# Placing the negated row maxima of an attention kernel: a TensorE transpose replaced by VectorE's 32x32 block transpose

## The chip, the cores and the metric

The kernel runs on one NeuronCore of a Trainium2 chip. The metric is the device time of one execution in microseconds (us), given as the median of several runs; lower is better. One further execution was recorded by the hardware profiler, and all traces below are of such an execution. TensorE appears in it as PE (matmuls) and PEld (weight loads), VectorE as DVE, ScalarE as ACT, GpSimd as POOL, and SyncE, which issues nearly all DMAs, as SP.

## The reference

All data are float32. One sequence of 2048 rows with 640 columns goes through two branches, which are mixed by a gate per row:

```python
g = sigmoid((x * gate_w).sum(-1))            # one number per row
q, k, v = split(x @ wqkv)                    # 32 heads of 20 columns
p = softmax(q @ k.T * 20 ** -0.5)            # per head, 2048 x 2048
a = (p @ v) @ wo
b = Cr @ (x @ Dr.T) - Ci @ (x @ Di.T)        # Fourier mixing, real part
out = g * a + (1 - g) * b
```

The weights are scaled so that scores are large: the exponential needs the maximum of each row subtracted. The change concerns how these maxima get into the matrix product whose result is exponentiated.

## The kernel before

**Units.** Attention runs in 32 units. A unit is a pair of heads and one half (1024) of the query rows. The two heads, h = 0 and h = 1, lie in the partitions from 0 and from 64 of the same tiles, so that two matmuls with few rows can run side by side. Scores are needed twice. The first pass (`s_mm`, L197, "m" in the order strings) computes a 128-query by 512-key block into a PSUM bank, and VectorE reduces it to 128 maxima (L199). The second pass (`score`, L949, "e") computes the block the other way round, 128 keys by 512 queries, and ScalarE exponentiates it (L951). The second pass uses 62 rows in place of 60: the rows 60 and 61 of a head's query stack hold the negated maximum of each query in two parts, a float32r value and the remainder, and the key stack holds ones there. So the matmul itself subtracts the maxima. Then the weights meet V (`av_step`, L556) in bursts of 16 or 24 matmuls.

**The chain of one unit.** `s_end` notes that a unit's first pass is done. `max_nm` (L213) reduces its maxima once more on VectorE to the tile `nm`: 128 partitions (the query within a block of 128) by 16 columns (head times 8 blocks), negated. `max_chain` has to lay these 128 x 16 numbers into rows of 1024 queries. Before, a matmul with the identity (L231) turns `nm` into 16 x 128 in a PSUM bank taken from the common rotation `bank()`, two VectorE operations (the helper `split`, L115 and L116) make the parts `m1` and `m2` of it, and `rows()` issues four DMAs on SP that place eight partitions of `m1` or `m2` as one row of 4 KB. From the first pass of a unit to its second there are 41 steps (`LEAD`), a step being one "e" for each of the two heads; a unit has 32 steps.

**What sets the order.** All engines work in program order; the order is written out by hand. In the long middle part, a cycle of six steps follows the second string of `ORDERS`: "e" and "m" are blocks of the two passes, "F" fills in matmuls of the Fourier branch (L635), and "B" is the burst, which first calls `run_extras` and `run_casts` (among them ScalarE's cast L113, whose remainder GpSimd then computes at L116), then the AV matmuls L556, and between or after them `max_chain`. The tuples behind the string tell which of the two heads comes first in a step: for "e" `(0, 0, 0, 1, 0, 1)`. Blocks of both passes take their PSUM banks in turn from five places of one rotation, so a block must wait until the block five places earlier has been read. The DMAs of `rows()` stand in SP's queue two steps after the chain; SP waits there, and everything behind it waits too.

**The parts of the span.** Up to about 217 us there are projections without chains; to about 600 us Fourier work of the hidden axis (L378) fills in, in cycles of four steps; to about 1650 us Fourier work of the sequence (L635), in cycles of six steps; then the output projection (L742). Units are numbered 0 to 31; unit 0's chain runs at 217 us, those of 1 to 7 stand in the second part, 8 to 28 in the third, 29 to 31 in the last.

Of the kernel before, what the change touches and what calls it, by code (L numbers as in the profile page):

```python
# [11 lines left out]
F32 = mybir.dt.float32  # L12
R = mybir.dt.float32r
# [6 lines left out]
P = 128  # L20
# [9 lines left out]
KROWS = 3 * DH  # L30
# [42 lines left out]
def f32(ap):  # L73
    return ap.bitcast(F32)
# [3 lines left out]
def mix_kernel(ctx: ExitStack, tc: tile.TileContext, xa, wqk, wb, cdft, wo, out):  # L78
    nc = tc.nc
    pe, act, dve, pool, sp = nc.tensor, nc.scalar, nc.vector, nc.gpsimd, nc.sync  # L80
    ctx.enter_context(tc.manual_schedule())

    def pools(**kw):
        return ctx.enter_context(tc.tile_pool(**kw))

    const = pools(name="const", bufs=1)
    small = pools(name="small", bufs=1)
# [13 lines left out]
    ident = const.tile([P, P], F32, name="ident")  # L101
# [9 lines left out]
    def split(dst1, dst2, src, e1, e2):  # L111
        if e1 is act:
            act.activation(dst1, src, AF.Copy)  # L113
        else:
            e1.tensor_copy(dst1, src)  # L115
        e2.tensor_tensor(dst2, src, f32(dst1), op=ALU.subtract)  # L116
# [8 lines left out]
    def place_tile(name):  # L125
        return ps_w.tile([P, 512], F32, name=name)

    def bank():
        places.rotate(-1)
        return place_tile(places[-1])  # L130
# [45 lines left out]
    def q_unit(n):  # L176
        p, u = VISITS[n]
        return third["q"] if p == 14 else qst[place(p)][:, u * (S // 2) : (u + 1) * (S // 2)]

    mx, nms, ends = {}, {}, []  # L180
    now, later = [-1], {}

    def at_step(i, fn):
        later.setdefault(i, []).append(fn)
# [16 lines left out]
    def s_end(i):  # L201
        n, s = divmod(i, 32)
        if n < NU and s == 31:
            if now[0] < 0:
                max_nm(n)
            else:
                ends.append(n)
        if s == 1 and 0 < n <= NU and now[0] < 0:
            max_chain(n - 1)
# [17 lines left out]

    def max_chain(n):
        q = q_unit(n)
        pt = bank()[:16, :P]  # L230
        pe.matmul(pt, nms.pop(n), ident, start=True, stop=True)  # L231
        m1 = small.tile([16, P], R, name="m1")
        m2 = small.tile([16, P], R, name="m2")
        split(m1, m2, pt, dve, dve)

        def rows():
            for h in range(2):
                b = 64 * h + KROWS
                sp.dma_start(f32(q[b : b + 1, :]), f32(m1[8 * h : 8 * h + 8, :]))
                sp.dma_start(f32(q[b + 1 : b + 2, :]), f32(m2[8 * h : 8 * h + 8, :]))  # L240

        if now[0] < 0:
            rows()
        else:
            at_step(now[0] + 2, rows)
# [578 lines left out]
    start = 4 * HID  # L824
# [130 lines left out]
    def burst(c):  # L955
        ready = any(n in nms for n in ends)
        for n in ends:
            if n not in nms:
                max_nm(n)
        k, _, i = phase(c)  # L960
        steps = 6 if k == 1 else 4
        run_extras(steps - 2)
        if k == 1:
            run_casts()
        for kt in range(i // 2, (i + steps) // 2):
            if ready and kt == (i + steps) // 2 - 1:
                max_chain(ends.pop(0))
            av_step(now[0], kt // NS, kt % NS, kt % NS == 0 and kt > i // 2)
        while ends:
            max_chain(ends.pop(0))  # L970
        if c in (HID - NS - 1, HID - 1):
            next_pool()
# [134 lines left out]
```

## Time and profile before

| | |
|---|---|
| Median of 3 runs | 1854.2 us (1853.94 to 1856.85) |
| Span of the profiled execution, first to last instruction | 1852.1 us |
| Mean granted TensorE clock | 0.999 |
| Busy: PE, PEld | 1844.1, 1365.3 us |
| Busy: DVE, ACT, POOL | 1379.7, 1357.0, 1003.6 us |
| Matmuls L231 | 64 records, 12.2 us |
| VectorE split of the turned maxima, L115 and L116 on `m` | 32 + 32, 8.8 + 8.9 us |
| Row DMAs L239 and L240 | 128 issues |

An engine's busy time is the time in which at least one of its instructions runs, waits inside an instruction included. A float32 matmul by the identity is recorded as two matmuls, hence 64 for 32 units. A row of a timeline gives the start in us from the span's start, the duration of the merged instructions, the engine, the line, and how many were merged; brackets give the idle time ahead and what ended it. A row of a group gives the count, then the minimum, median and maximum duration in ns. SP's instructions are issues of DMAs; their durations are the time the issuing takes, not the transfer.

### The profile page before, as it was taken

The numbers are of one execution on the slowest core, as the hardware profiler recorded it, in microseconds if no ns is written. First come the engines' busy times: TensorE is split into PE (matmuls) and PEld (weight loads), VectorE is DVE, ScalarE is ACT, GpSimd is POOL, SyncE is SP. The second block draws the span as 40 slices with busy tenths as digits, with TensorE's granted clock in tenths as the row PEclk, the third lists the DMA queues.
The fourth block names the chain that finished last, engine by engine and source line by source line (L and its number), as shares of the span: only waits on it lengthen the run. The fifth ranks groups of instructions, "written<-read, shape, count | busy, mean of one in ns | idle before, by whom it ended". The sixth has DMA issues, their size and how long they took to land.

```text
span 1852.1 us, 44874 instructions
## 1 busy us (share of the span) xinstructions
PE 1844.1 (100%) x17638; PEld 1365.3 (74%) x17638; DVE 1379.7 (74%) x2309; ACT 1357.0 (73%) x2645; POOL 1003.6 (54%) x832
## 2 busy tenths in 40 slices
PE   9999999999999999999999999999999999999998
PEld 8988777676776777777777777777777777776666
DVE  3044458888787888888888888888888888888853
ACT  4222258878787888888788888888888877778885
POOL 4334432121136676344677788655668767645644
PEclk9999999999999999999999999999999999999999
DMA  7744341222135574636566586646475856531233
GB/s 236 173 136 157 136 126 56 79 64 67 58 92 149 200 215 148 157 118 194 177 201 227 159 261 197 192 140 183 130 235 189 246 163 206 178 91 55 82 99 109
DMA packets 178771, 281.61 MB, mean 152 GB/s; under 512 B 44811, under 2 KB 113547, under 8 KB 178559
## 3 DMA queue, kind: packets, MB, share of 16 engines
q1 hardware_dynamic: 177599, 276.77, 49.1%
q0 software_dynamic: 960, 1.97, 0.6%
q8 instruction: 138, 2.26, 0.5%
q14 instruction: 74, 0.61, 0.1%
HBM read 214.61 MB, written 63.52 MB: 150 GB/s over the span
## 4 chain that ended last, share of the span: by engine, by line
PE 99%; DMA 0%; DVE 0%; ACT 0%; POOL 0%; SPq 0%; issue 0%; POOLq 0%; ACTq 0%
PE ps L556 25%; PE yp L635 19%; PE ps L949 17%; PE ps L197 14%; PE yp L378 7%; PE ps L119 4%; PE ps L120 4%; PE ps L121 4%; PE yp L742 3%; DMA p<-in_xa 0%; PE ps L231 0%; DVE mx L199 0%; PE ps L1041 0%; POOL x L1010 0%; PE yp L1062 0%
## 5 line engine op out<-in xcount | busy, mean ns | idle before, releaser
L199 DVE TENSOR_REDUCE mx<-ps 128x1 f32<-128x512 f32 x2048 | 1280.6, 684 | 305.8 <-PE ps L197 235.8
L951 ACT ACTIVATE p<-ps 128x512 f32<-128x512 f32 x2048 | 1055.1, 612 | 282.4 <-PE ps L197 159.3
L949 PE MATMUL ps<-qst,kst 62*128 62x512 f32 x1920 | 727.7, 406 | 0.2
L197 PE MATMUL ps<-kst,qst 60*128 60x512 f32 x1920 | 664.3, 409 | 0.0
L635 PE MATMUL yp<-x,part 64*128 64x320 f32 x5376 | 628.1, 306 | 0.0
L635 PEld LDWEIGHTS yp<-x,part 64*128 64x128 f32 x5376 | 601.7, 186 | 5.2
L556 PE MATMUL ps<-p,v 128*21 128x512 f32 (+1 forms) x4096 | 482.0, 595 | 0.0
L116 POOL TENSOR_TENSOR part<-raw,part 128x1024 fp32r<-128x1024 f32 (+1 forms) x128 | 287.4, 2246 | 338.3 <-ACT part L113 322.4
L949 PEld LDWEIGHTS ps<-qst,kst 62*128 62x128 f32 x1920 | 341.3, 185 | 155.5 <-DVE mx L199 86.4
L197 PEld LDWEIGHTS ps<-kst,qst 60*128 60x128 f32 x1920 | 323.3, 184 | 11.8 <-issue 4.2
L556 PEld LDWEIGHTS ps<-p,v 128*21 128x21 f32 (+1 forms) x4096 | 104.8, 101 | 236.1 <-issue 228.6
L378 PE MATMUL yp<-wb,x 64*128 64x320 f32 x1920 | 223.9, 307 | 0.0
L378 PEld LDWEIGHTS yp<-wb,x 64*128 64x128 f32 x1920 | 209.8, 186 | 6.5 <-ACT raw L388 0.2
L389 POOL TENSOR_TENSOR raw<-raw 128x320 f32<-128x320 f32 x64 | 55.6, 869 | 267.0 <-ACT raw L388 210.0
L515 POOL TENSOR_TENSOR raw<-raw,raw 128x1024 f32<-128x1024 f32 x77 | 187.4, 2434 | 1.5 <-DMA raw<-in_cdft 1.5
L113 ACT ACTIVATE part<-raw 128x1024 fp32r<-128x1024 f32 (+2 forms) x121 | 123.4, 1020 | 2.0 <-DMA raw<-in_wqk 1.9
L742 PE MATMUL yp<-x,part 64*128 64x320 f32 x768 | 102.2, 308 | 0.0
L116 POOL TENSOR_TENSOR x<-araw,x 128x320 fp32r<-128x320 f32 x112 | 97.4, 877 | 1.3
L338 ACT ACTIVATE p<-ps 128x512 f32<-128x512 f32 x40 | 23.7, 597 | 100.1 <-PE ps L121 97.1
L742 PEld LDWEIGHTS yp<-x,part 64*128 64x128 f32 x768 | 92.0, 186 | 1.3
L119 PE MATMUL ps<-x,part 128*128 128x512 f32 x200 | 79.9, 400 | 0.5 <-ACT x L113 0.3
L120 PE MATMUL ps<-x,part 128*128 128x512 f32 x200 | 78.6, 393 | 0.4 <-DVE x L116 0.4
(101 smaller groups left out, 1364.2 us busy)
## 6 DMA issues: line engine op xcount, KB each, us to landing
raw<-in_cdft SPq DMA_DIRECT2D x192, 512.0 KB
araw<-a_scr SPq DMA_DIRECT2D x192, 160.0 KB
qk_scr<-p SPq DMA_DIRECT2D x40, 512.0 KB
kst<-qk_scr SPq DMA_DIRECT2D x84, 160.0 KB
qst<-qk_scr SPq DMA_DIRECT2D x84, 160.0 KB
yt<-y_scr SPq DMA_DIRECT2D x80, 160.0 KB
a_scr<-raw SPq DMA_DIRECT2D x64, 160.0 KB
y_scr<-yt SPq DMA_DIRECT2D x64, 160.0 KB
```

Of the source, the lines that this page charges most:

```text
L116: e2.tensor_tensor(dst2, src, f32(dst1), op=ALU.subtract)
L119: pe.matmul(ps, st1, mv1, start=first, stop=False)
L120: pe.matmul(ps, st1, mv2, start=False, stop=False)
L197: pe.matmul(ps, q[b : b + KROWS, qt * P : (qt + 1) * P], k[b : b + KROWS, kc * 512 : (kc + 1) * 512], start=True, stop=True)
L199: return lambda: dve.tensor_reduce(mx[n][:, h, qt, kc : kc + 1], ps, axis=AX.X, op=ALU.max)
L378: pe.matmul(yp[h][:, :HE], x[r, xz, d, cs], w[r, wz, d, :HE], start=d == 0 and z == 0, stop=d == ND - 1 and z == 2)
L515: pool.tensor_tensor(raws[0], raws[0], raws[1], op=ALU.add if PRODUCTS[n][0][1][0] > 0 else ALU.subtract)
L556: pe.matmul(t[32 * j : 32 * j + m, :], v[:, r : r + m], pp[qc][:, h, :], start=kt == 0, stop=kt == NS - 1)
L635: pe.matmul(yp[h][:, :HE], c[r, cz, cs], a[r, az], start=s == 0 and z == 0, stop=s == NS - 1 and z == 2)
L742: pe.matmul(yp[h][:, :HE], o[oz][r], wos[d, hf][r, wz], start=d == 0 and z == 0, stop=end)
L949: pe.matmul(pt, k[b : b + KROWS + 2, kt * P : (kt + 1) * P], q[b : b + KROWS + 2, qc * 512 : (qc + 1) * 512], start=True, stop=True)
L951: act.activation(pts[n, kt, qc][:, h], pt, AF.Exp, scale=float(DH) ** -0.5)
```

## The change

The maxima are no longer turned by TensorE. `max_chain` splits `nm` where it lies, in SBUF with its 128 partitions, into a tile `mt` of 128 x 32 (head, part, block of queries), and VectorE's block transpose turns each of the four 32 x 32 squares into `mtt`. A partition of `mtt` then holds 32 queries of one head, part and block. Eight DMAs place them: for each head h and each group b of 32 partitions, sixteen pieces of 128 bytes go to the two rows of the head.

```diff
     def max_chain(n):
         q = q_unit(n)
-        pt = bank()[:16, :P]
-        pe.matmul(pt, nms.pop(n), ident, start=True, stop=True)
-        m1 = small.tile([16, P], R, name="m1")
-        m2 = small.tile([16, P], R, name="m2")
-        split(m1, m2, pt, dve, dve)
+        t, tt = [small.tile([P, 32], F32, name=name) for name in ("mt", "mtt")]
+        parts = t.rearrange("p (h z c) -> p h z c", h=2, z=2).bitcast(R)
+        split(parts[:, :, 0], parts[:, :, 1], nms.pop(n).rearrange("p (h c) -> p h c", h=2), dve, dve)
+        dve.transpose(tt, t)
 
         def rows():
             for h in range(2):
-                b = 64 * h + KROWS
-                sp.dma_start(f32(q[b : b + 1, :]), f32(m1[8 * h : 8 * h + 8, :]))
-                sp.dma_start(f32(q[b + 1 : b + 2, :]), f32(m2[8 * h : 8 * h + 8, :]))
+                dst = f32(q[64 * h + KROWS : 64 * h + KROWS + 2, :]).rearrange("z (t b c) -> z t b c", t=8, b=4)
+                for b in range(4):
+                    r = 32 * b + 16 * h
+                    sp.dma_start(dst[:, :, b], tt[r : r + 16])
```

Outside the 32 chains the order of the instructions on every engine is the same; the rotation of banks advances by one place less per unit. The next rows show VectorE's queue at the chain of unit 10, from `nm` to the first reductions behind the chain (L199 reads a block's bank, `ps`). Before:

```order
L213 TENSOR_REDUCE nm<-mx 128x16
L199 TENSOR_REDUCE mx<-ps_10498 128x1
L199 TENSOR_REDUCE mx<-ps_10501 128x1
L199 TENSOR_REDUCE mx<-ps_10507 128x1
L199 TENSOR_REDUCE mx<-ps_10510 128x1
L115 CAST m_10526<-ps_10524 16x128
L116 TENSOR_TENSOR m_10527<-ps_10524,m_10526 16x128
L199 TENSOR_REDUCE mx<-ps_10539 128x1
```

Now:

```order
L213 TENSOR_REDUCE nm<-mx 128x16
L199 TENSOR_REDUCE mx<-ps_10528 128x1
L199 TENSOR_REDUCE mx<-ps_10531 128x1
L199 TENSOR_REDUCE mx<-ps_10537 128x1
L199 TENSOR_REDUCE mx<-ps_10540 128x1
L115 CAST mt<-nm 128x2x8
L116 TENSOR_TENSOR mt<-nm,mt 128x2x8
L233 STREAM_TRANSPOSE mtt<-mt 128x32
L199 TENSOR_REDUCE mx<-ps_10568 128x1
```

The chain keeps its place among the reductions; it is three instructions in place of two, and its inputs are `nm` and `mt` in SBUF in place of a PSUM bank `ps`.

SP's queue at the same unit, where `m_10526` and `m_10527` are the parts `m1` and `m2`. Before:

```order
L580 DMA r_scr<-lc 128x16
L239 DMA qst_89<-m_10526 1x8x128
L240 DMA qst_89<-m_10527 1x8x128
L239 DMA qst_89<-m_10526 1x8x128
L240 DMA qst_89<-m_10527 1x8x128
L510 DMA raw<-in_cdft 128x1024
L584 DMA rb<-r_scr 32x512 x4
```

Now:

```order
L580 DMA r_scr<-lc 128x16
L240 DMA qst_89<-mtt 2x8x32 x8
L510 DMA raw<-in_cdft 128x1024
L584 DMA rb<-r_scr 32x512 x4
L775 DMA y_scr<-m 128x320 x2
L891 DMA kst_86<-qk_scr 20x4x512
```

Eight issues stand where four stood, h = 0 first, and the loads behind them are unchanged.

TensorE's queue at the same place (L556 the burst, `ps_10524` the bank of the turned maxima). Before:

```order
L556 MATMUL ps_9893<-p,v 21x512 x8
L231 MATMUL ps_10524<-ident,nm 16x128
L556 MATMUL ps_9893<-p,v 21x512 x4
L949 MATMUL ps_10536<-qst_88,kst_86 128x512
L197 MATMUL ps_10539<-kst_87,qst_89 128x512
```

Now the row L231 is gone and the twelve rows of L556 stand together; the blocks behind them follow in the same order.

## The prediction

> **What bounds the kernel now.** First the page's busy times and its chain of waits:
>
> ```profile
> PE 1844.1 (100%) x17638; PEld 1365.3 (74%) x17638; DVE 1379.7 (74%) x2309; ACT 1357.0 (73%) x2645; POOL 1003.6 (54%) x832
> PE 99%; DMA 0%; DVE 0%; ACT 0%; POOL 0%; SPq 0%; issue 0%; POOLq 0%; ACTq 0%
> ```
>
> TensorE sets the end. A busy PE is no proof, since its ends are modelled, so I read PE's timeline next, for the starts of the bursts L556 in cycles of six steps, without a chain (672.19 to 681.49, 728.47 to 737.76) and with one.
>
> ```profile
> 672.19 2.77 PE L556 MATMUL ps<-p,v 128*21 128x512 f32 x24
> 681.49 2.77 PE L556 MATMUL ps<-p,v 128*21 128x512 f32 x24
> 684.08 0.38 PE L231 MATMUL ps<-ident,nm 128*16 128x128 f32 x2
> 691.26 0.63 PE L556 MATMUL ps<-p,v 128*21 128x512 f32 x4
> ...
> 728.47 2.77 PE L556 MATMUL ps<-p,v 128*21 128x512 f32 x24
> 737.76 1.91 PE L556 MATMUL ps<-p,v 128*21 128x512 f32 x16
> 739.49 0.27 PE L231 MATMUL ps<-ident,nm 128*16 128x128 f32 x1
> 740.66 0.49 PE L949 MATMUL ps<-qst,kst 62*128 62x512 f32 x1
> 742.24 0.39 PE L949 MATMUL ps<-qst,kst 62*128 62x512 f32 x1
> 745.55 0.39 PE L949 MATMUL ps<-qst,kst 62*128 62x512 f32 x1
> 747.26 1.06 PE L556 MATMUL ps<-p,v 128*21 128x512 f32 x8
> ```
>
> A cycle without a chain takes 9.30 us (681.49 - 672.19), a fixed beat; with a chain inside the burst 9.50 (747.26 - 737.76), with one behind the burst 9.77 (691.26 - 681.49). So PE has no slack that could take up a new wait, and each L231 costs it a time that can be read off.
>
> **What the change removes.** The transposes' rows:
>
> ```profile
> L231 PE MATMUL ps<-ident,nm x64: 272/273/283, 217.3 to 1782.3; 128*16 128x128 f32 x64
>   DVE nm L213: 8.4, 18
>   DVE mx L199: 4.3, 14
> ```
>
> The 14 are chains inside a burst (units 8, 10, 11, 13 and so on), 0.20 us each, 2.8 in all. The 18 are seven behind bursts of six steps (9, 12 and so on to 27; 0.47, so 3.3), one of unit 0 with two waits, and ten behind bursts of four steps (1 to 7, 29 to 31), for which I take 0.20 too: 2.3. The 0.47 holds 0.20 for the matmuls; the rest comes later in that cycle, from the turned maxima's place in the bank rotation, which goes too. **Gain: 8.4 us.**
>
> **What it puts on VectorE.** The split now has 16 elements in each of 128 partitions. Neighbours by size:
>
> ```profile
> L457 DVE TENSOR_SCALAR ngate<-gate x1: 177/177/177, 121.3 to 121.3; 128x16 f32<-128x16 f32 x1
> L213 DVE TENSOR_REDUCE nm<-mx x32: 207/216/221, 217.0 to 1779.8; 128x16 f32<-128x64 f32 x32
> L1057 DVE COPY rb<-lc x1: 427/427/427, 1836.5 to 1836.5; 128x512 f32<-128x512 f32 x1
> 739.91 0.28 DVE L115 CAST m<-ps 16x128 fp32r<-16x128 f32 x1
> 740.23 0.28 DVE L116 TENSOR_TENSOR m<-ps,m 16x128 fp32r<-16x128 f32 x1
> 741.23 1.91 DVE L199 TENSOR_REDUCE mx<-ps 128x1 f32<-128x512 f32 x3 [0.72 <-PE ps L197]
> ```
>
> I take 0.17 for the cast, 0.18 for the subtraction, 0.20 for the block transpose (no row has one: 0.18 to 0.43, near the small ones) and 0.04 behind each, together 0.67 us against 0.59 before. By itself that is nothing: VectorE idles 0.72 us behind the chain of unit 10.
>
> But two operations change the memory they read, and the trace has a row on what that can cost. First the group of a subtraction with both inputs in SBUF, then two of its members and what GpSimd ran beside them:
>
> ```profile
> L116 DVE TENSOR_TENSOR wb<-raw,wb x8: 815/1166/2151, 18.1 to 117.7; 128x966 fp32r<-128x966 f32 x4, 128x644 fp32r<-128x644 f32 x4
> 115.58 2.15 DVE L116 TENSOR_TENSOR wb<-raw,wb 128x966 fp32r<-128x966 f32 x1 [3.28 <-ACT wb L113]
> 115.40 1.30 POOL L116 TENSOR_TENSOR p<-p 128x512 fp32r<-128x512 f32 x1
> 19.83 1.35 DVE L116 TENSOR_TENSOR wb<-raw,wb 128x644 fp32r<-128x644 f32 x1 [0.50 <-ACT wb L113]
> 18.40 2.09 POOL L116 TENSOR_TENSOR p<-p 128x512 fp32r<-128x512 f32 x1
> ```
>
> An operation that takes about 1.17 us (the group's median) took 2.15: GpSimd's ended at 116.70, and from there VectorE took 1.03. The second pair repeats it (GpSimd's end 20.49, VectorE's 21.18, 0.69 later, for a shape whose shortest took 0.82). So VectorE's subtraction from two SBUF inputs stands still until GpSimd's operation ends. Before, the subtraction had a PSUM input; now both are in SBUF. The Trainium skill ("SBUF — State Buffer", section "Who interferes with whom") says the same of VectorE instructions with two SBUF inputs, and says it of casts too, since they may run in a two-port mode; it calls the lock exclusive for a whole instruction. The two pairs agree on the subtraction; no run here shows a cast. By that rule the cast waits as well, which is the mechanism of the first rival below.
>
> What GpSimd does at the chains:
>
> ```profile
> 636.61 2.38 POOL L116 TENSOR_TENSOR part<-raw,part 128x1024 fp32r<-128x1024 f32 x1 [3.21 <-ACT part L113]
> 638.95 0.88 POOL L116 TENSOR_TENSOR x<-araw,x 128x320 fp32r<-128x320 f32 x1
> 683.00 2.37 POOL L116 TENSOR_TENSOR part<-raw,part 128x1024 fp32r<-128x1024 f32 x1 [1.70 <-ACT part L113]
> 739.27 2.38 POOL L116 TENSOR_TENSOR part<-raw,part 128x1024 fp32r<-128x1024 f32 x1 [5.75 <-ACT part L113]
> 889.02 2.37 POOL L116 TENSOR_TENSOR part<-raw,part 128x1024 fp32r<-128x1024 f32 x1 [2.56 <-ACT part L113]
> 891.36 2.42 POOL L515 TENSOR_TENSOR raw<-raw,raw 128x1024 f32<-128x1024 f32 x1
> ```
>
> The burst itself starts the cast that this L116 waits for, so 2.4 us of GpSimd's work fall on the chain in units 8 to 27. In unit 10 VectorE is ready at 739.91 and held until 741.65; the chain ends at 742.32. Behind it stand the reductions L199. The first takes about 0.65 us, to 742.97, and frees the bank that the fourth block of the second pass needs. That block stands 4.48 us behind the burst's start (742.24), now 4.28 (742.04): PE loses 0.93. The same sum for unit 9 (burst 681.49, GpSimd until 685.37: bank free 686.69, wanted 685.77) gives 0.92, for unit 8 (its burst five cycles before 681.49, four of 9.30 and one of 9.50, so at 634.79; GpSimd until 638.99: 640.31 against 639.07) 1.24. **Loss: seven units like 8, 8.7 us; seven like 9, 6.4; six like 10, 5.6.** Unit 28 lies behind the last of them. In units 1 to 6 the chain follows `nm` at once and I count nothing; unit 7 up to 0.9 goes into the range.
>
> **What it puts on SP.** Row issues of units 10 and 28, and other issues:
>
> ```profile
> 740.22 0.65 SPq L239 DMA_DIRECT2D qst<-m  x1
> 742.34 0.64 SPq L240 DMA_DIRECT2D qst<-m  x1
> ...
> 1638.81 0.66 SPq L239 DMA_DIRECT2D qst<-m  x1
> 1640.89 1.22 SPq L240 DMA_DIRECT2D qst<-m  x1
> ...
> L239 SPq DMA_DIRECT2D qst<-m x60: 634/646/775, 219.9 to 1784.3; - x60
> L891 SPq DMA_DIRECT2D kst<-qk_scr x84: 273/331/1472, 254.6 to 1556.6; - x84
> 1644.16 0.39 PE L949 MATMUL ps<-qst,kst 62*128 62x512 f32 x1
> ```
>
> Four issues stand 0.71 apart. Eight in this form, the nearest in kind (a few SBUF partitions to rows of SBUF), take 7 x 0.71 + 0.64 = 5.6 us; at the cheap end, L891's 0.33 and 0.05 between, 3.0. Landing is not shown: in unit 28 the last issue ends at 1642.11 and the block that needs it runs at 1644.16, so 0 to 2.05 us; I take 1.2. In units 10, 13, 16, 19, 22, 25 and 28 the next unit's first block comes early (745.55 in unit 10), and by the tuple `(0, 0, 0, 1, 0, 1)` it is of h = 1, whose rows are issued last: it waits for all eight. In unit 10: 742.35 + 5.6 + 1.2 = 749.15, against 745.55 - 0.20 + 0.93 = 746.28: PE stands for 2.9 us, six times 17.2. In unit 28 the first issue stands at 1638.81; with the chain 0.6 us longer, as in a short hold by GpSimd, it comes at 1639.45: 1646.25 against 1643.96, 2.3. **Loss: 19.5 us**; at cheap issues 1 to 2. The other units have two to four times the room.
>
> Behind the rows wait loads of `in_cdft` (L510), late by some 5 us. Their remainders are ready 8 us before PE uses them (unit 10's cycle: 741.65, used a cycle later), so that is hidden; uncovered it would cost up to 5 us a unit. Extra semaphore waits of PE (four DMAs a head in place of two) I count as nothing: its queue runs ahead.
>
> **Sum.** -8.4 + 20.7 + 19.5 = +32 us on the span of 1852.1, so 1884. The median lies 2.1 us above that span, launch and spread included: 1854.2 + 32 = **1886 us**.
>
> **Rivals.**
>
> *GpSimd goes again between cast and subtraction.* If the cast is held as the subtraction is, GpSimd's next operation is waiting when the cast ends, and the subtraction waits for that too: 2.42 us in units 13, 16, 22 and 25 (as at 891.36) and in two of the others (26, 27), 0.88 in all but 10 and 19 of the rest (as at 638.95). That adds 6 x 2.42 + 12 x 0.88 = 25: 1911 us, with cheap issues 1893. For it: GpSimd's rows follow each other without a gap. Against: no row shows a cast held.
>
> *Neither is held, faster.* Operations of 0.2 us might pass where long ones did not. Then the chain ends at 740.58 in unit 10, and everything hangs on the issues: they must be done and landed by 745.35, so stand less than (745.35 - 1.2 - 740.6)/8 = 0.44 us apart. With L891's 0.38 the whole 8.4 us is left: 1846 us. With 0.71, seven units lose 2.0 and it comes to 1860. Against it: two pairs of rows.
>
> *Cheap issues, with the hold as forecast.* -8.4 + 20.7 + 2 = +14: 1869 us.
>
> *GpSimd wins every time* while it has work in a row, VectorE losing 3 to 5 us a chain: over 1915.
>
> **How the numbers follow.** The forecast (hold once, dear issues) 0.35; hold once with cheap issues 0.15; GpSimd between 0.27 (a third of it cheap); no hold 0.16, half with cheap issues; GpSimd every time 0.07. Left out of the range 1858 to 1911 are the faster case, the last one and some of the dear end. A measurement of this kernel tells about 0.2% (3.7 us) from no change. Faster by more: 0.09; within: 0.04 (issues between the two prices); slower: 0.87.
>
> **What would show it.** Right: L116 on `mt` in units 8 to 27 with durations near 1.5 us (or the cast, if that is held), ending about 0.2 us behind GpSimd's L116; cycles with a chain over 10 us; first blocks waiting for DMAs on `qst` in one unit of three. L231 gone and cycles at 9.30 with chains would show the gain alone. Wrong: `mt` operations at 0.2 us each, or eight issues within 3 us of each other.

## The result

| | before | after |
|---|---|---|
| Median | 1855.8 us (1853.9 to 1857.1) | 1916.65 us (1915.3 to 1922.1) |
| Span of the profiled execution | 1852.1 us | 1913.5 us |
| Mean granted TensorE clock | 0.999 | 0.993 |

The change makes the kernel slower: ratio 1.0339, 95% interval 1.0325 to 1.0354, or 61 us. The forecast was 1886 us, 32 slower, with a range that ended at 1911. The direction was right and the size about half of what came.

The page of the changed kernel, its busy times and its chain of waits by engine:

```profile
PE 1854.6 (97%) x17574; PEld 1368.6 (72%) x17574; DVE 1432.0 (75%) x2341; ACT 1362.6 (71%) x2645; POOL 1002.8 (52%) x832
PE 85%; DVE 8%; DMA 3%; SPq 2%; issue 1%; POOL 1%; ACT 0%; POOLq 0%; DVEq 0%; ACTq 0%
```

Before, TensorE held 99% of the chain; now VectorE, DMAs and SP hold 13% of it. VectorE has 52 us more of busy time, although its new instructions are small. The groups of instructions on the tile `mt` (count, then minimum, median and maximum in ns) show where that went:

```profile
L115 DVE CAST mt<-nm x32: 164/1502/1915, 222.1 to 1843.2; 128x16 fp32r<-128x16 f32 x32
L116 DVE TENSOR_TENSOR mt<-nm,mt x32: 174/784/2282, 222.3 to 1843.6; 128x16 fp32r<-128x16 f32 x32
L233 DVE STREAM_TRANSPOSE mtt<-mt x32: 211/211/214, 222.5 to 1843.9; 128x32 f32<-128x32 f32 x32
```

A cast and a subtraction of 16 elements per partition take 0.16 and 0.17 us when nothing holds them, and 1.50 and 0.78 at the median. The transpose takes 0.211 each time. The timeline of unit 13 shows both holds, GpSimd's rows beside VectorE's, then SP's and TensorE's:

```profile
904.63 2.77 PE L556 MATMUL ps<-p,v 128*21 128x512 f32 x24
906.68 1.85 DVE L115 CAST mt<-nm 128x16 fp32r<-128x16 f32 x1
908.57 2.28 DVE L116 TENSOR_TENSOR mt<-nm,mt 128x16 fp32r<-128x16 f32 x1
910.88 0.21 DVE L233 STREAM_TRANSPOSE mtt<-mt 128x32 f32<-128x32 f32 x1
911.02 1.84 DVE L199 TENSOR_REDUCE mx<-ps 128x1 f32<-128x512 f32 x3
...
906.13 2.37 POOL L116 TENSOR_TENSOR part<-raw,part 128x1024 fp32r<-128x1024 f32 x1 [2.51 <-ACT part L113]
908.46 2.36 POOL L515 TENSOR_TENSOR raw<-raw,raw 128x1024 f32<-128x1024 f32 x1
...
911.12 5.27 SPq L240 DMA_DIRECT2D qst<-mtt  x8
...
911.72 0.50 PE L949 MATMUL ps<-qst,kst 62*128 62x512 f32 x1 [2.63 <-DVE mx L199]
917.53 0.47 PE L949 MATMUL ps<-qst,kst 62*128 62x512 f32 x1 [0.70 <-DMA qst<-mtt]
919.30 1.91 PE L556 MATMUL ps<-p,v 128*21 128x512 f32 x16
```

The cast begins at 906.68, while GpSimd runs L116, and ends at 908.53, just behind GpSimd's end at 908.50. GpSimd's next operation has begun at 908.46 by then; the subtraction ends at 910.85, just behind that one (910.82). It is the same everywhere: of the 64 casts and subtractions of the changed kernel 43 take over 0.3 us, and each of these ends 0.03 to 0.04 us behind an end of a GpSimd operation; to the ends of ScalarE's operations they stand in no fixed distance. TensorE stands 2.63 us for a bank that L199 frees late, then 0.70 for the rows. The cycle takes 14.67 us (919.30 - 904.63) against 9.49 before. The two waits give 3.3 of the 5.2 us; the windows of that cycle give the rest (columns: window, then length, busy time and instructions of PE, PEld, DVE, ACT and POOL, then the granted clock, the DMA share and GB/s):

```profile
908.74:912.15 3.41, 0.78 (x10) 0.47 (x9) 3.38 (x4) 0.77 (x2) 2.08 (x1) 1.00 0.00 0
912.15:915.56 3.41, 3.41 (x25) 3.41 (x24) 2.29 (x5) 2.37 (x4) 0.00 (x0) 0.50 0.02 3
904.63:919.30 14.67, 11.34 (x98) 8.26 (x96) 11.87 (x16) 7.68 (x14) 4.69 (x2) 0.88 0.13 36
```

From 912.15 on, behind the stall, the granted clock is 0.50 for 3.41 us. Over the cycle it is 0.88, so (1 - 0.88) x 14.67 = 1.8 us are lost to the clock (half of 3.41 is 1.7). Such a stretch follows six stalls of the changed kernel (in units 13, 16, 22, 25 and 27, and the one between units 6 and 7, below), about 10 us in all.

Two stalls stand where the prediction saw none, between the chains of units 6 and 7 (+4.5 us) and behind that of unit 7 (+2.4). For the second, SP's and ScalarE's rows, before:

```profile
593.49 0.90 SPq L510 DMA_DIRECT2D raw<-in_cdft  x2
594.68 0.33 SPq L891 DMA_DIRECT2D a_scr<-raw  x1
599.42 0.77 ACT L388 ACTIVATE raw<-yp 128x320 f32<-128x320 f32 x2 [0.18 <-DMA a_scr<-raw]
```

and after:

```profile
595.75 3.88 SPq L240 DMA_DIRECT2D qst<-mtt  x6
601.99 0.90 SPq L510 DMA_DIRECT2D raw<-in_cdft  x2
602.99 0.38 SPq L891 DMA_DIRECT2D a_scr<-raw  x1
607.84 0.77 ACT L388 ACTIVATE raw<-yp 128x320 f32<-128x320 f32 x2 [2.90 <-DMA a_scr<-raw]
```

The store `a_scr<-raw` frees one of three `raw` tiles, and ScalarE needs it to empty TensorE's banks. The burst of this cycle is at 598.39 before and at 604.09 after, so the store goes from 3.7 to 1.1 us ahead of it: it stands behind the row issues in SP's queue.

How long a cycle of six steps with a chain takes, from burst to burst (a cycle without one stays at 9.30 in both), and the two stalled cycles:

| cycle with the chain of | before | after |
|---|---|---|
| unit 11 (like 8, 14, 17, 20, 23) | 9.48 | 11.13 |
| unit 12 (like 9, 15, 18, 21, 24) | 9.79 | 10.85 |
| unit 10 (like 19) | 9.50 | 12.62 |
| unit 13 (like 16, 22, 25) | 9.49 | 14.67 |
| units 26, 27, 28 | 9.51, 9.76, 9.52 | 12.63, 13.74, 11.38 |
| between units 6 and 7; behind 7 | 6.50; 8.45 | 11.04; 10.89 |

Units 8 to 28 sum to +53 us, the stalls around unit 7 to +7.5 (0.5 of it in that unit's own cycle), and the chains of units 1 to 6 in cycles of four steps, which do lose L231, to -1.2; all cycles together make +59. The first burst comes 1.9 us later in this profile, at 259.3 us; in the profiles shown here such starts vary from 256.5 to 259.9 us, without the two in which unit 0's chain itself loses time.

### The profile page after: what moved, and what is told of

Read it like the earlier page. It is cut to its first block, busy times and chain, and to the rows that moved or that the text cites. A ratio compares the mean times of both kernels' runs of the same rounds, so it can differ in the third digit from the quotient of the medians.

```text
span 1913.5 us, 44979 instructions
## 1 busy us (share of the span) xinstructions
PE 1854.6 (97%) x17574; PEld 1368.6 (72%) x17574; DVE 1432.0 (75%) x2341; ACT 1362.6 (71%) x2645; POOL 1002.8 (52%) x832
## 4 chain that ended last, share of the span: by engine, by line
PE 85%; DVE 8%; DMA 3%; SPq 2%; issue 1%; POOL 1%; ACT 0%; POOLq 0%; DVEq 0%; ACTq 0%
PE ps L556 20%; PE yp L635 17%; PE ps L949 15%; PE ps L197 12%; PE yp L378 6%; DVE mx L199 4%; PE ps L119 4%; PE ps L120 4%; PE ps L121 4%; PE yp L742 3%; DVE mt L115 2%; SPq L240 2%; DVE mt L116 1%; DMA a_scr<-raw 1%; DMA yt<-y_scr 1%
## 5 line engine op out<-in xcount | busy, mean ns | idle before, releaser
L199 DVE TENSOR_REDUCE mx<-ps 128x1 f32<-128x512 f32 x2048 | 1279.4, 682 | 322.9 <-PE ps L197 265.8
L635 PE MATMUL yp<-x,part 64*128 64x320 f32 x5376 | 642.4, 309 | 1.4 <-ACT raw L388 1.4
L116 POOL TENSOR_TENSOR part<-raw,part 128x1024 fp32r<-128x1024 f32 (+1 forms) x128 | 287.8, 2248 | 368.0 <-ACT part L113 340.7
L556 PE MATMUL ps<-p,v 128*21 128x512 f32 (+1 forms) x4096 | 479.2, 595 | 0.0
L556 PEld LDWEIGHTS ps<-p,v 128*21 128x21 f32 (+1 forms) x4096 | 103.9, 101 | 245.4 <-issue 238.3
L742 PE MATMUL yp<-x,part 64*128 64x320 f32 x768 | 102.4, 309 | 0.0
L116 POOL TENSOR_TENSOR x<-araw,x 128x320 fp32r<-128x320 f32 x112 | 97.5, 879 | 1.3
```

Of the source, the lines that this page charges most:

```text
L199: return lambda: dve.tensor_reduce(mx[n][:, h, qt, kc : kc + 1], ps, axis=AX.X, op=ALU.max)
L556: pe.matmul(t[32 * j : 32 * j + m, :], v[:, r : r + m], pp[qc][:, h, :], start=kt == 0, stop=kt == NS - 1)
L635: pe.matmul(yp[h][:, :HE], c[r, cz, cs], a[r, az], start=s == 0 and z == 0, stop=s == NS - 1 and z == 2)
L742: pe.matmul(yp[h][:, :HE], o[oz][r], wos[d, hf][r, wz], start=d == 0 and z == 0, stop=end)
```

## Experiments

Two theories stand at the start. **A**: VectorE is held by GpSimd at the cast and again at the subtraction, which is most of the loss; the eight issues are the rest. **B**: the eight issues on SP are the loss, and the hold is hidden. Ratios are against the kernel before, with 95% intervals.

### Eight issues alone

```diff
-                sp.dma_start(f32(q[b : b + 1, :]), f32(m1[8 * h : 8 * h + 8, :]))
-                sp.dma_start(f32(q[b + 1 : b + 2, :]), f32(m2[8 * h : 8 * h + 8, :]))
+                for k in range(2):
+                    r = 8 * h + 4 * k
+                    c = slice(512 * k, 512 * k + 512)
+                    sp.dma_start(f32(q[b : b + 1, c]), f32(m1[r : r + 4, :]))
+                    sp.dma_start(f32(q[b + 1 : b + 2, c]), f32(m2[r : r + 4, :]))
```

> The kernel before (matmul with the identity, split from PSUM) with each of its four row transfers cut into two halves, so that eight issues stand where four stood; nothing else changes. Theory A (VectorE held by GpSimd costs about two thirds of the loss, the eight issues the rest): the issues alone make the first second-pass blocks of units 10, 13, 16, 19, 22, 25 and 28 wait, about 1.4 us each (last issue ends in unit 10 at 740.22 + 7 x 0.66 + 0.64 = 745.5, 1.2 until landed, wanted at 745.35), and perhaps the two stalls behind late stores of raw tiles (7 us): 1865 to 1872 us. Theory B (the issues are nearly the whole loss, the hold is hidden): 61 + 8 = about 69 us more, 1925 us. Theory C (small pieces of 128 bytes make the transfers slow; the issues do nothing): 1856.

Measured: 1858.8 us, ratio 1.0015 (1.0005 to 1.0025), below what either A or B gave. B falls for these issues; for those of the changed kernel the run without a hold will decide. The issues are dear, as forecast: in the chain of unit 10 they stand 0.62 apart, and the last ends at 748.85.

```profile
743.86 0.61 SPq L242 DMA_DIRECT2D qst<-m  x1
...
748.28 0.57 SPq L243 DMA_DIRECT2D qst<-m  x1
...
749.22 0.40 PE L952 MATMUL ps<-qst,kst 62*128 62x512 f32 x1
```

The first block runs on time at 749.22, 0.37 behind the last issue. The expectation had it wait for all eight, but a block of 512 queries needs only the first half of a row in this cut, so it waits for nothing issued after 747.62. In the changed kernel each transfer holds pieces of all eight blocks of queries, and the block does need all. So this run prices SP's share without the waits for rows: the two stalls around unit 7 (7.34 and 10.40 against 6.50 and 8.45) are 2.8 us, the whole of its loss.

### The cast held, no second operation

```diff
-        split(parts[:, :, 0], parts[:, :, 1], nms.pop(n).rearrange("p (h c) -> p h c", h=2), dve, dve)
+        dve.tensor_copy(parts[:, :, 0], nms.pop(n).rearrange("p (h c) -> p h c", h=2))
+        dve.memset(f32(parts[:, :, 1]), 0.0)
```

> The changed kernel with the subtraction of the chain replaced by a fill of the second part with zeros; the remainder of the maxima is left out. So VectorE can be held once, at the cast, but there is no second operation that reads two SBUF inputs. Theory A (the cast is held, then GpSimd goes once more and holds the subtraction): the cast keeps its median of about 1.5 us, the second wait goes, 0.8 us in most units and 2.3 in some, so 20 to 28 us less than the changed kernel: 1889 to 1897. Theory B (the loss is in the issues): no change, 1917. If the zero fill is itself held as the subtraction was: also 1917, with its duration showing it.

Measured: 1884.7 us, ratio 1.0161 (1.0144 to 1.0178), 32 us less than the changed kernel.

```profile
L232 DVE CAST mt<-nm x32: 165/1498/1871, 222.7 to 1818.3; 128x16 fp32r<-128x16 f32 x32
L233 DVE MEMSET mt<- x32: 72/72/72, 222.8 to 1818.5; 128x16 f32 x32
```

The cast is held as before, and the fill behind it never. It comes out 4 us below theory A's range. Cycles like unit 13's fall from 14.7 to 12.4 us, 1.7 of it because the clock stays at 1.00 there; that was in neither theory. In units 10 and 19 it is the other way round: half clock follows a wait of 2.2 us for the rows, and their cycles grow from 12.6 to 13.8.

### No hold at all

```diff
-        split(parts[:, :, 0], parts[:, :, 1], nms.pop(n).rearrange("p (h c) -> p h c", h=2), dve, dve)
+        dve.tensor_reduce(parts[:, :, 0], nms.pop(n).rearrange("p (h c o) -> p h c o", h=2, o=1), axis=AX.X, op=ALU.max)
+        dve.memset(f32(parts[:, :, 1]), 0.0)
```

> The changed kernel with the cast done as a reduction over an axis of one element (same numbers, another form of instruction) and the subtraction replaced by a fill with zeros; the remainder of the maxima is left out. Place, transpose and eight row transfers are as in the changed kernel. Theory A: the reduction runs 0.2 us beside GpSimd, as the reduction to nm does; what is left is the matmul with the identity saved (8.4 us) against the eight issues in units 10, 13 and so on (last issue 740.6 + 7 x 0.66 + 0.64, 1.2 until landed, 1.7 to 2 us late, seven times) and up to 7 us at the late stores: 1858 to 1868 us. Theory B (issues alone): 1917.

Measured: 1859.7 us, ratio 1.0024 (1.0015 to 1.0033), inside A's range. The group of the reduction, then SP and the first block that waits, in unit 10:

```profile
L232 DVE TENSOR_REDUCE mt<-nm x32: 157/166/171, 219.7 to 1787.8; 128x16 fp32r<-128x16 f32 x32
...
741.84 5.27 SPq L241 DMA_DIRECT2D qst<-mtt  x8
...
748.30 0.46 PE L950 MATMUL ps<-qst,kst 62*128 62x512 f32 x1 [1.18 <-DMA qst<-mtt]
```

The same copy, at the same place, beside the same GpSimd work, takes 0.17 us as a reduction. The cycles of units 11 and 12 fall to 9.30 and 9.29, which is L231's whole cost gained. What is left is the wait for rows in units 10, 13, 16, 19, 22, 25 and 28 (10.7 to 10.8 us a cycle, some 10 us in all) and the stalls around unit 7. The three medians give prices: the first hold 1884.7 - 1859.7 = 25 us, the second 1916.65 - 1884.7 = 32. The spans of the three profiled executions (1858.1, 1888.6 and 1913.5) split the same sum into 30 and 25, so the sum is surer than its parts. The eight issues are those of the changed kernel here, so B falls for good.

The Trainium skill ("SBUF — State Buffer", section "Who interferes with whom") says that on trn2 a reduction never contends with GpSimd, while a cast can and a subtraction with both inputs in SBUF does. The 0.166 here against 1.50 and 0.78 of the changed kernel agree.

### Four turns, four transfers, the holds kept

```diff
-        dve.transpose(tt, t)
+        for b in range(4):
+            dve.transpose(tt[:, 32 * b : 32 * b + 32], t[32 * b : 32 * b + 32, :])
...
-                for b in range(4):
-                    r = 32 * b + 16 * h
-                    sp.dma_start(dst[:, :, b], tt[r : r + 16])
+                for z in range(2):
+                    b = 64 * h + KROWS + z
+                    r = 16 * h + 8 * z
+                    sp.dma_start(f32(q[b : b + 1, :]), tt[r : r + 8])
```

> The changed kernel with the split kept where it is, but four block transposes of 32 x 32 whose results stand side by side in 32 partitions, so that four row transfers of 8 x 512 bytes serve, as in the kernel before. The complete computation. Theory A: the holds stay (1.5 us cast, 0.8 us subtraction); the chain grows by three short transposes (0.2 to 0.6 us in some 20 units, 4 to 12 us); the first blocks of units 10, 13 and so on wait some 2.6 us less (7 times) and the stalls behind late stores shrink (up to 7 us): 1893 to 1908 us. Theory B (the issues are the loss): 1856 - 8 = 1848 us. Theory C (pieces of 128 bytes): 1848 too, and then the eight issues of 512-byte pieces are cheap.

Measured: 1924.0 us, ratio 1.0363 (1.0347 to 1.0378); neither theory had it slower than the changed kernel. What A said of SP holds: the two cycles around unit 7 are back at 6.31 and 8.48 us. But the chain is 0.6 us longer, and cycles like unit 12's take 13.09. The turns, then TensorE and the windows in unit 9:

```profile
L235 DVE STREAM_TRANSPOSE mtt<-mt x128: 199/199/204, 222.5 to 1852.7; 32x32 f32<-32x32 f32 x128
...
692.01 0.50 PE L951 MATMUL ps<-qst,kst 62*128 62x512 f32 x1 [1.80 <-DVE mx L199]
...
694.00:695.00 1.00, 1.00 (x10) 1.00 (x7) 0.69 (x1) 0.28 (x2) 0.45 (x1) 0.50 0.04 8
685.75:698.78 13.03, 11.22 (x98) 8.16 (x96) 11.01 (x21) 8.31 (x16) 7.18 (x5) 0.87 0.42 145
```

A 32 x 32 turn costs 0.199 us, hardly less than four in one instruction. The wait in unit 9 is 1.80 us where the changed kernel has 1.57, and this time the clock goes to 0.50: (1 - 0.87) x 13.03 = 1.7 us more. The mean clock of the run is 0.987 against 0.993 in the changed kernel; 0.006 of 1922 us is 11.5 us, which is more than the two differ by. Theory C, that the pieces of 128 bytes are the loss, falls with this run, whose pieces are of 512 bytes.

### The same chain from PSUM

```diff
-        split(parts[:, :, 0], parts[:, :, 1], nms.pop(n).rearrange("p (h c) -> p h c", h=2), dve, dve)
+        nm = bank()[:, :16].rearrange("p (h c) -> p h c", h=2)
+        dve.tensor_reduce(nm, nms.pop(n).rearrange("p (h c o) -> p h c o", h=2, o=1), axis=AX.X, op=ALU.max)
+        split(parts[:, :, 0], parts[:, :, 1], nm, dve, dve)
```

> The changed kernel with nm first laid into a PSUM bank of the common rotation by a reduction over an axis of one element, so that cast and subtraction read PSUM as in the kernel before; place, transpose and eight row transfers as in the changed kernel, the whole computation. Theory A (the loss is the hold of cast and subtraction while both read SBUF): neither is held; the chain is about 0.5 us longer than in the run without a hold, which adds 0.5 to the wait for rows in seven units, and the bank costs up to 0.27 in seven others: 1859.7 + 3.5 + 1.9 = 1865, 1861 to 1869 us. Rival D (what counts is that the subtraction's remainder is computed at all, or the place of the chain): 1885 or more.

Measured: 1869.1 us, ratio 1.0083 (1.0065 to 1.0101), at the upper end of A's range.

```profile
L115 DVE CAST mt<-ps x32: 173/174/176, 219.9 to 1793.4; 128x16 fp32r<-128x16 f32 x32
L116 DVE TENSOR_TENSOR mt<-ps,mt x32: 173/174/175, 220.1 to 1793.6; 128x16 fp32r<-128x16 f32 x32
```

Not one of 64 operations is held once the source is a PSUM bank. So it is the SBUF input that counts, and rival D falls. The rows leave some 0.4 us later than in the run without a hold, and cycles like unit 10's take 11.1 to 11.25.

### GpSimd moved instead of the chain

```diff
-        if k == 1:
+        if k == 1 and ends:
+            at_step(now[0] + 2, run_casts)
+        elif k == 1:
             run_casts()
```

> The changed kernel with the chain untouched (its operations, its place among VectorE's instructions, SBUF inputs, eight transfers); only in the cycles with a chain ScalarE's casts L113, which release GpSimd's subtractions L116, are made behind the second block of the next cycle in place of ahead of the burst, so that GpSimd starts some 3 to 4 us later. The whole computation. Theory A (the holder is GpSimd's operation that runs at that moment): cast and subtraction fall to 0.17 us in most units 8 to 28 and the cycles of units like 9 to 9.3 us plus what ScalarE's casts cost between the exponentials (0 to 1.5 us in 21 units); units like 10 keep 1.4 us for the rows; the stalls of units 6 and 7 stay: 1860 to 1890 us. Rival E (something else on VectorE's side holds them): the medians stay at 1.5 and 0.8 us, 1910 or more.

Measured: 1885.7 us, ratio 1.0170 (1.0151 to 1.0189). The chain is that of the changed kernel, instruction by instruction.

```profile
L115 DVE CAST mt<-nm x32: 161/174/932, 220.8 to 1810.5; 128x16 fp32r<-128x16 f32 x32
L116 DVE TENSOR_TENSOR mt<-nm,mt x32: 174/175/799, 221.0 to 1810.9; 128x16 fp32r<-128x16 f32 x32
...
690.55 2.37 POOL L116 TENSOR_TENSOR part<-raw,part 128x1024 fp32r<-128x1024 f32 x1 [5.58 <-ACT part L113]
...
691.73 0.50 PE L949 MATMUL ps<-qst,kst 62*128 62x512 f32 x1 [1.12 <-ACT p L951]
```

With GpSimd's L116 3.6 to 3.9 us later the medians fall to 0.174 and 0.175 us. ScalarE's casts move too, so this run alone would leave two holders; together with the ends of the held operations, which follow GpSimd's and not ScalarE's, it shows that GpSimd is the holder. The casts of ScalarE, now among the exponentials, make TensorE wait 1.1 us in units like 9 and 0.8 in units like 8, which is the larger part of what keeps the time above that of the run without a hold.

### The chain early, with one transpose or with four

```diff
+        while ends:
+            max_chain(ends.pop(0))
         k, _, i = phase(c)
...
-                    for n in ends:
-                        max_nm(n)
+                    while ends:
+                        max_nm(ends[0])
+                        max_chain(ends.pop(0))
```

(The calls of `max_chain` inside and behind the burst are gone.)

> The changed kernel with the whole chain (cast, subtraction, transpose) put directly behind nm, ahead of the burst or at its start, where GpSimd has no work, in place of inside or behind the burst; the operations are the same and read SBUF. The whole computation. Theory A (the hold is GpSimd's): cast and subtraction take 0.17 us each in nearly all units, the rows leave 2 to 4 us earlier so that no first block waits, and what is left is the gain of 8.4 us less the stall by late stores (0 to 4): 1847 to 1853 us. Rival E (the operations themselves are slow on this layout, whatever GpSimd does): 1900 or more. Rival F (0.6 us of VectorE put ahead of the burst make blocks wait for their banks): 1855 to 1862.

Measured: 1870.5 us, ratio 1.0085 (1.0068 to 1.0103). All three lines missed. Where A's reason holds, its numbers do too: cycles like those of units 10 and 13 take 9.30 and 9.29, hold and wait for rows both gone. But where `nm` is made at the burst's start, GpSimd is there first, in unit 9 by 0.9 us:

```profile
689.18 1.49 DVE L115 CAST mt<-nm 128x16 fp32r<-128x16 f32 x1
690.70 0.79 DVE L116 TENSOR_TENSOR mt<-nm,mt 128x16 fp32r<-128x16 f32 x1
...
688.26 2.38 POOL L116 TENSOR_TENSOR part<-raw,part 128x1024 fp32r<-128x1024 f32 x1 [1.69 <-ACT part L113]
```

These cycles keep 10.85 us, and unit 27's takes 14.96.

The same early place with the four turns of the earlier run:

> As the run before it, with the chain directly behind nm, but with four block transposes whose results stand side by side and four row transfers of 8 x 512 bytes. The whole computation. Theory A: the longer chain (1.2 us) finds no GpSimd operation, the four issues fewer on SP take the late stores away: 1846 to 1851 us. Rival F (VectorE time put ahead of the burst): 0.6 us more a unit than with one transpose, so 10 us or more slower than that run.

Measured: 1881.5 us, ratio 1.0144 (1.0129 to 1.0159), 11 us slower than with one transpose, as rival F had it, though mostly in the cycles that are still held: unit 12's takes 12.97 us, again with a stall of 1.8 us and half the clock behind it, while unit 11's grows from 9.59 to 9.89 and unit 10's not at all. The cycles around unit 7 are at 6.16 and 8.48.

### Both mended

`nm` reduced straight into a PSUM bank, and the chain early everywhere (by the moves of `max_chain` shown above):

```diff
-        nms[n] = small.tile([P, 16], F32, name="nm", bufs=2)
+        nms[n] = bank()[:, :16]
```

> nm is reduced straight into a PSUM bank and cast, subtraction and transpose stand directly behind it, ahead of the burst or at its start; eight row transfers. The whole computation. Theory A (both terms are now gone: no input pair in SBUF, so no hold by GpSimd in any unit, and rows that leave 2 to 4 us earlier): the cycles of units 8 to 28 take 9.30 us, the gain of 8.4 us stands, less the two stalls behind late stores of raw tiles (units 6 and 7: 0.5 to 1.6 and 2.1 to 3.7 us): 1849 to 1853 us. Rival: the bank taken ahead of the burst makes blocks wait for theirs, up to 0.3 us in 21 units: 1855 to 1859.

Measured: 1861.5 us, ratio 1.0042 (1.0027 to 1.0056), above A's range and the rival's too. The cycles with a hold or a wait for rows are gone, all 21 at 9.3 us except one (9.5). But the cycle ahead of each early chain now takes 9.86 or 9.68 in place of 9.30; here the one ahead of unit 8's burst, from burst to burst:

```profile
630.19 2.77 PE L567 MATMUL ps<-p,v 128*21 128x512 f32 x24
640.07 2.77 PE L567 MATMUL ps<-p,v 128*21 128x512 f32 x24
```

A bank of the rotation is taken there, between blocks that need it. Fourteen such cycles lose some 6.7 us. Unit 0's chain, far ahead, loses as well: TensorE waits 2.0 us at 219.88 for the bank of its `nm`, and 3.41 us at half clock follow.

With four turns and four transfers for units 0 to 7 alone, to take SP's lateness away:

```diff
+        four = n < 8
```

> As the run before it, but units 0 to 7 use four block transposes and four row transfers in place of one and eight, so that SyncE is free earlier where raw tiles are stored. The whole computation. Theory A: the stalls behind late stores go (cycles of 6.2 and 8.5 us there, as in the runs with four transfers), the chains of units 1 to 7 grow by 0.6 us of VectorE time, which nothing waits for: 1846 to 1849 us, 0.3% to 0.5% faster than the kernel before. If those stalls come from something else than SyncE's issues: as the run before it.

Measured: 1858.3 us, ratio 1.0018 (1.0009 to 1.0027). The cycles around unit 7 are back at 6.16 and 8.46, so those stalls were SP's issues; the 14 cycles and the loss at unit 0 (a wait of 2.0 us and half clock behind it) remain, and with a first burst 3 us later than in the run before it the time misses A's range by 9 us.

The last version takes a bank only where `nm` is made at the burst:

```diff
-    def max_nm(n):
-        nms[n] = bank()[:, :16]
+    def max_nm(n, psum=False):
+        nms[n] = bank()[:, :16] if psum else small.tile([P, 16], F32, name="nm", bufs=2)
...
+        four = 0 < n < 8
...
             if n not in nms:
-                max_nm(n)
+                max_nm(n, True)
```

> As the run with four transfers for the first units, but nm goes to a PSUM bank only where it is made at the burst (units like 9 and 1 to 7); in units like 8 and 10 the chain stands directly behind nm with nm in SBUF, where GpSimd has little to do. The whole computation. Theory A: no bank is taken ahead of the burst, so the 14 cycles that stood at 9.68 or 9.88 us fall to 9.30 (up to 9.6 where a short GpSimd operation holds the cast): 1846 to 1851 us, 0.2% to 0.4% faster than the kernel before. If the bank was not the cause: as that run, 1858.

Measured: 1848.6 us against 1856.8 for the kernel before on the same chip, ratio 0.9961 (0.9948 to 0.9973): faster than both kernels. The page, and the groups of the chain:

```profile
PE 1836.6 (99%) x17574; PEld 1360.5 (74%) x17574; DVE 1384.2 (75%) x2362; ACT 1355.7 (73%) x2645; POOL 1004.6 (54%) x832
...
L115 DVE CAST mt<-ps x17: 173/173/174, 289.4 to 1775.5; 128x16 fp32r<-128x16 f32 x17
L116 DVE TENSOR_TENSOR mt<-ps,mt x17: 173/174/175, 289.6 to 1775.7; 128x16 fp32r<-128x16 f32 x17
L115 DVE CAST mt<-nm x15: 163/175/609, 220.1 to 1631.6; 128x16 fp32r<-128x16 f32 x15
L116 DVE TENSOR_TENSOR mt<-nm,mt x15: 174/175/796, 220.3 to 1631.8; 128x16 fp32r<-128x16 f32 x15
```

The 14 cycles ahead of an early chain are at 9.3 us again, save those ahead of units 19 and 25, so the bank was their cause. (Unit 0 is back at the changed kernel's form too, far ahead of these cycles; its wait of 2.0 us and the half clock behind it are gone, which is some 3.7 us of what this run gains on the one before it.) Twenty of the 21 cycles with a chain are at 9.3; the one at 10.18 (unit 17), and the two ahead of units 19 and 25 (10.53 and 10.64), lose 3.4 us together. In the latter two ScalarE waits 1.7 and 1.1 us for GpSimd's `araw` (L549), and TensorE then 0.8 and 0.9 for the exponentials; why GpSimd is late there is open. Without these cycles the stretch from the first burst to the last, 1575.0 us before and 1570.2 now, would have gained 8.2 us, close to the 8.4 that L231 was counted at.

The cycles of the main runs side by side (us):

| cycle | cast held | no hold | four turns | PSUM | casts late | early | last version |
|---|---|---|---|---|---|---|---|
| unit 11 | 10.32 | 9.30 | 11.74 | 9.32 | 10.57 | 9.59 | 9.30 |
| unit 12 | 10.01 | 9.29 | 13.09 | 9.37 | 10.94 | 10.85 | 9.31 |
| unit 10 | 13.76 | 10.76 | 10.81 | 11.14 | 10.96 | 9.30 | 9.30 |
| unit 13 | 12.37 | 10.70 | 15.18 | 11.10 | 10.89 | 9.29 | 9.30 |
| units 6 to 7 | 7.77 | 7.02 | 6.31 | 8.08 | 7.22 | 8.34 | 6.16 |
| behind 7 | 11.98 | 12.19 | 8.48 | 10.56 | 10.58 | 12.17 | 8.45 |

## Why the prediction was right and wrong

- **What bounds the kernel, and the gain of 8.4 us: right.** TensorE has no slack, and each hold shows up in a cycle. Where nothing else is lost, the cycles of units like 11 and 12 fall from 9.50 and 9.77 to 9.30, as read from the rows of L231.
- **VectorE's prices: right.** Cast, subtraction and transpose were taken at 0.17, 0.18 and 0.20 us; unheld they take 0.17, 0.17 and 0.211.
- **One hold a chain: this step failed.** The forecast took from two pairs of rows that a subtraction with two SBUF inputs is held, and let the cast pass because no row showed one held. The cast is held, and by the time it ends GpSimd has begun its next operation, which holds the subtraction. That is the first rival (1911 us), given 0.27 against 0.35 for the forecast. The number of holds was wrong by one, and the second measures 32 us by the medians, 25 by the profiled executions, stretches of half clock included; that rival had priced it at 25. (The 20.7 us of the one hold let the whole chain of 0.67 us follow it, which is the case when the cast is the one held.)
- **The case that the forecast did describe came out near it, in part by luck.** One hold and eight dear issues is the run with the cast held alone: 1884.7 us against 1886. In its cycles the hold costs some 17 us (what units 8 to 28 take above 9.30, less waits for rows and half clock) in place of 20.7, and TensorE waits 14.6 us for rows in place of 19.5. Against these 8.6 us too many stand 8.2 that were in no term: the two stalls around unit 7 (4.8) and half clock behind two waits (3.4).
- **The wait for rows, 19.5 us: mechanism right, size too large.** The issues stand 0.66 apart in place of 0.71, and the rows land 1.2 us behind the last issue, as taken. Seven units wait, those that were named. Without a hold they lose 1.4 us each, some 10 us. With two holds the two terms do not add: in unit 13 the block is late already, and only 0.70 us is left for the rows; the seven waits of the changed kernel are 9.6 us together. The rival "neither is held" with dear issues said 1860, and the run without a hold gave 1859.7; two errors of about 4 us offset each other in it, the waits for rows smaller and the stalls around unit 7 larger.
- **The loads behind the rows "hidden": wrong for what else stands in that queue.** I looked at the loads of `in_cdft` and not at the stores `a_scr<-raw`, which free a tile that ScalarE waits for. The two stalls cost 7 us in the changed kernel, and are gone in all four versions with four issues there (6.2 to 6.3 and 8.5 us).
- **Not in the sum at all: the clock.** Six stalls are followed by half the clock, about 1.7 us each, 10 us; one of them is part of the 7 us above. The first rival's 1911 lacked this and those stores, some 15 us together, and came within 6 us of the 1916.65 because its waits for rows were 10 us too large.
- **The fourth rival, GpSimd every time for 3 to 5 us a chain, did not occur as told.** The two holds together are 2.3 us at the median (1.50 + 0.78) and reach 4.1 in units like 13.

## What to carry to other kernels

Before an operation of VectorE is moved from a PSUM source to SBUF, look at what GpSimd runs at that moment and at what stands next in its queue: two short dependent operations can each wait for a whole GpSimd operation, whatever their own size. In this kernel reading from PSUM, copying by a reduction, or moving the work to where GpSimd is idle took the wait away, and the last must be checked at every place of the schedule. When issues are added to a queue, price every item that comes behind them, the stores that free buffers as well as the loads.

## What the runs showed of the hardware that I had not expected

**A stall of TensorE can cost more than its length.** Behind stalls of 2.6 to 2.8 us the granted clock was 0.50 for 3.41 us. The length alone does not decide: of waits of 1.8 us some were followed by it (unit 9 of the four turns) and others not, in the changed kernel one of 2.2 us (unit 10) and one of 3.0 (unit 26) were not, and in the run without a hold one of 1.3 us behind unit 7 was. The traces show that it matters where a stall falls. The stretches of half clock of one profile start whole multiples of 3.413 us apart; in the changed kernel they start at 567.40, 912.15, 1069.16, 1383.19, 1540.20 and 1642.60, which are 101, 46, 92, 46 and 30 such steps. In the step ahead of each, TensorE was busy for only 0.61 to 1.25 of the 3.41 us (0.78 in unit 13, in the windows above). The wait of 3.0 us in unit 26 falls across a border of these steps, at 1591.40, and each of the two keeps more work:

```profile
1587.98:1591.40 3.42, 2.00 (x20) 1.36 (x16) 3.39 (x3) 1.57 (x3) 3.42 (x2) 1.00 0.00 0
1591.40:1594.81 3.41, 1.82 (x20) 1.82 (x22) 3.30 (x7) 1.30 (x3) 1.50 (x2) 1.00 0.01 1
```

In all profiles of these runs where such a stretch tells the steps (between 240 and 1815 us), a step at full clock was followed by half clock each time that TensorE was busy for less than 47% of it, and never when for more than 64%; between these both occurred. No run was made to move a stall on purpose. The Trainium skill ("TensorE: Matmul & The Clock Gate", section "What's actually happening") describes two clock states, half and full, set by a window of 3413 ns that runs free of the program. The 0.50, the 3.41 us and the steps of 3.413 us agree with that. It asks for an idle window of about 3.4 us before the clock falls; here steps in which TensorE was busy for up to nearly half the time were enough, and the measurement decides.

**Transposes.** One instruction that turns four 32 x 32 blocks takes 0.211 us, and one that turns a single block 0.199, in all runs and beside any GpSimd work: the transpose was never held.
